# One-input POOL operations beside attention: normalising by a scalar, rounding for w3 and w_out, low parts on DVE

## The chip, the core and the metric

One core of a Trainium2 chip runs the whole kernel as one program. Five engines each work through their own list of instructions in order and wait for one another by semaphores: TensorE (PE, with weight loads listed as PEld), VectorE (DVE), ScalarE (ACT), GpSimd (POOL) and SyncE (SP), which here only starts DMAs. The metric is the device time of one execution in microseconds (us), smaller being better.

## The reference

Causal attention over 2 batches of 12 heads (448 positions, 64 wide), then two dense blocks on its 896 x 768 result:

```
scores = q @ k.T / 8, masked above the diagonal
x  = softmax(scores) @ v              # heads side by side: 896 x 768
h  = ((x @ w1) * (x @ w2)) @ w3 @ moe_w_out      # 768 -> 1024 -> 1024 -> 768
t  = h @ w_in                                    # 768 -> 2048
y  = (t * clip(t + 3, 0, 6) / 6) @ moe2_w_out    # 2048 -> 768
```

The weights arrive as 64-bit floating-point numbers and q, k, v are turned into 32-bit ones. The kernel has to return y in 32 bits.

## The kernel before, in words

**Weights.** A 64-bit weight is read as two 32-bit words, a high word (index 1) and a low word (index 0) side by side in a raw tile, `raw[:, :size, 0 or 1]`. `bits` (line 262) makes a 32-bit float of the pair in four steps: ACT scales the high words as floats (line 270); the top bits of the low words are brought down by 29 places, either on DVE by a shift (line 277) or, with `shifted`, on ACT by an activation with a scale and a bias (line 273); DVE merges the high words' mantissa bits (line 279) and then the sign bit (line 281). The 32-bit float stands in the low words' place, every other word of the tile. `split` (line 249) makes two parts of it: ACT rounds it to the format that TensorE multiplies fast (HI, line 252), and the difference from the unrounded value is the low part (LO, line 255). A product is then three multiplications, HI by HI, HI by LO and LO by HI.

**Units.** A unit is one 128-wide slice of a weight. For w3 (8 units of 1024 columns, tile `w3r`, parts `w`) and for moe_w_out, called wr (8 units of 768 columns, tile `wrr`, parts `wr`), the list `POOLED` puts the low part's subtraction on POOL; for the others it is on DVE. `convert` (line 284) does a unit, `fetch` (line 229) loads one. Three raw tiles and four tiles of parts go round; the wr parts have tiles of their own.

**Order of work.** The product w3 · moe_w_out ("pw", line 543, 16 half slices through `weights_product`) does not depend on attention and is run beside it. After it come eight steps "pa" that multiply x by w1 and w2 (line 686; `combine` forms sums of weight blocks for them, partly with two-input additions on POOL, line 320), then px (line 760), pg (line 625) and po (line 801).

**Attention** goes by 12 units of two heads, each in seven row tiles t = 6 … 0 of 64 · (t + 1) columns. For each tile PE forms scores (line 407), DVE masks them and takes the row bound (line 410), ACT takes the exponential and the row sum (line 414). `normalise` (line 419) is done in three groups (t = 6 and 5; 4 and 3; 2, 1 and 0): DVE adds a small constant to the sums and takes the reciprocal (lines 425, 426), and POOL multiplies each row tile by it (line 433). PE transposes the result in blocks (line 455), ACT and DVE copy it out (lines 463, 467), PE multiplies by v (line 480) and ACT and DVE write the parts of x (lines 497, 498).

**What sets the order.** A planner (`Plan.issue`) fixes each engine's order when the program is built: it plays the operations through with a price for each (`act`, `dve`, `pool`: a constant plus a price per column) and at each step gives an engine, among the operations that are ready, the one of lowest rank. Attention ranks by unit, conversion beside it by PACE · n, and pw at BESIDE + n, so that it fills in. The prices know nothing of one engine slowing another. What runs on the chip keeps the planned order even where the times turn out otherwise.

Of the kernel before, what the change touches and what calls it, by code (L numbers as in the profile page):

```python
# [14 lines left out]
ALU = mybir.AluOpType  # L15
# [18 lines left out]
POOLED = ("wr", "w3")  # L34
# [120 lines left out]
def attention_moe_moe2(ctx: ExitStack, tc, q, k, v, w1, w2, w3, w_out, v_in, v_out, out):  # L155
# [8 lines left out]
    nc = tc.nc  # L164
# [3 lines left out]
    P = 128  # L168
    T = 64
# [9 lines left out]
    HI, LO = 0, 1  # L179

    def f32(ap):
        return ap.bitcast(F32)
# [37 lines left out]
    def act(n, sb=False):  # L220
        return (0.29 if sb else 0.16) + n * 0.000833

    def dve(n):
        return 0.155 + n * 0.00104

    def pool(n):
        return 0.15 + n * 0.0023

    def fetch(plan, n, rank):
        if n >= len(units):  # L230
            return
        w, kt, m, name = units[n]
        size = kt * P
        if name == "w2":
            raw = plan.tile(lambda: later["t"].tile([P, KD * P, 2], U32, tag="raw2", name=f"{name}r{m}", bufs=2),
                            "raw2", 2, (done,))
            raw2s.append(raw)
        else:
            raw = plan.tile(lambda: ws.tile([P, KF * P, 2], U32, tag="raw", name=f"{name}r{m}", bufs=RAWS), "raw", RAWS)
        raws[n] = (raw, size)  # L240
        flat = lambda: raw[:, :size].rearrange("p f t -> p (f t)")
        if name == "wp":
            plan.op("sp", size * 0.0015, lambda: nc.sync.dma_start(flat()[:, :size], product_of[m].bitcast(U32)),
                    reads=[made], writes=[raw], rank=rank)
        else:
            plan.op("sp", size * 0.0029, lambda: nc.sync.dma_start(flat(), w[m].bitcast(U32)),
                    writes=[raw], rank=rank)

    def split(plan, hl, at_, size, x, reads, rank, eng="dve"):

        key = ("h", at_)
        plan.op("act", act(size, True), lambda: nc.scalar.copy(hl[:, HI, at_:at_ + size], x()),
                reads=reads, writes=[hl.at(("h", at_))], rank=rank)
        e = nc.gpsimd if eng == "pool" else nc.vector
        plan.op(eng, pool(size) if eng == "pool" else dve(size), lambda: e.tensor_tensor(  # L255
            hl[:, LO, at_:at_ + size], x(), f32(hl[:, HI, at_:at_ + size]), ALU.subtract),
            reads=[*reads, hl.at(("h", at_))], writes=[hl.at(("l", at_))], rank=rank)

    def parts(name, m):
        return plan.tile(lambda: ws.tile([P, 2, KF * P], F32R, tag="hl", name=f"{name}{m}", bufs=HLS), "hl", HLS)  # L260

    def bits(plan, raw, size, rank, shifted=False):

        hi = lambda: raw[:, :size, 1]
        lo = lambda: raw[:, :size, 0]
        hb, lb = raw.at("h"), raw.at("l")

        plan.op("act", act(size, True), lambda: nc.scalar.mul(hi().bitcast(F32), hi().bitcast(F32), 2.0 ** -112),  # L270
                writes=[hb], rank=rank)
        if shifted:
            plan.op("act", act(size, True), lambda: nc.scalar.activation(
                lo(), lo(), AF.Copy, bias=THIRD[1], scale=THIRD[0]), writes=[lb], rank=rank)
        else:
            plan.op("dve", 0.16 + size * 0.00052,
                    lambda: nc.vector.tensor_single_scalar(lo(), lo(), 29, ALU.logical_shift_right),
                    writes=[lb], rank=rank)
        plan.op("dve", dve(size), lambda: nc.vector.scalar_tensor_tensor(  # L279
            lo(), hi(), 3, lo(), ALU.logical_shift_left, ALU.bitwise_or), reads=[hb], writes=[lb], rank=rank)  # L280
        plan.op("dve", dve(size), lambda: nc.vector.scalar_tensor_tensor(  # L281
            lo(), hi(), 0x80000000, lo(), ALU.bitwise_and, ALU.bitwise_or), reads=[hb], writes=[lb], rank=rank)

    def convert(plan, n, rank):
        if n >= len(units):
            return
        w, kt, m, name = units[n]
        if name == "w1":
            return
        raw, size = raws.pop(n)  # L290
        if name == "w2":
            combine(plan, m, raws.pop(n - 1)[0], raw, rank)
            return
        if name == "wr":
            hl = plan.tile(lambda: wrp.tile([P, 2, KD * P], F32R, tag="wr", name=f"wr{m}", bufs=KF), "wr", KF)
        else:
            hl = parts(name, m)
        hls[n] = hl
        if name == "wp":
            x = lambda: f32(raw[:, :].rearrange("p f t -> p (f t)")[:, :size])  # L300
            split(plan, hl, 0, size, x, [raw], rank)
            return
        bits(plan, raw, size, rank)
        split(plan, hl, 0, size, lambda: f32(raw[:, :size, 0]), [raw.at("l")], rank,
              "pool" if name in POOLED else "dve")

    def combine(plan, f, r1, r2, rank):


        size, h = KD * P, KD * P // 2  # L310
        bits(plan, r1, size, rank, True)
        low = lambda r, i, k=1: f32(r[:, i * h:(i + k) * h, 0])
        high = lambda r, i, k=1: f32(r[:, i * h:(i + k) * h, 1])
        first, second, third, fourth = (parts(f"{c}", f) for c in ("wa", "wb", "wc", "wd"))
        split(plan, first, 0, size, lambda: low(r1, 0, 2), [r1.at("l")], rank)
        bits(plan, r2, size, rank, True)

        def add(eng, dst, reads, write, a, b, op):
            e = nc.gpsimd if eng == "pool" else nc.vector
            plan.op(eng, pool(h) if eng == "pool" else dve(h), lambda: e.tensor_tensor(dst(), a(), b(), op),  # L320
                    reads=reads, writes=[write], rank=rank)

        L1, L2, H1, H2 = r1.at("l"), r2.at("l"), r1.at("h"), r2.at("h")
        add(ADDS[0], lambda: high(r2, 0), [L2], H2, lambda: low(r2, 0), lambda: low(r2, 1), ALU.add)
        add(ADDS[1], lambda: high(r2, 1), [L1, L2], H2, lambda: low(r1, 0), lambda: low(r2, 0), ALU.subtract)
        add(ADDS[2], lambda: high(r1, 0), [L1, H2], H1, lambda: high(r2, 0), lambda: low(r1, 0), ALU.subtract)
        add(ADDS[3], lambda: high(r1, 1), [L1], H1, lambda: low(r1, 1), lambda: high(r1, 0), ALU.subtract)
        split(plan, third, 0, h, lambda: high(r1, 0), [H1], rank)
        split(plan, second, 0, size, lambda: high(r2, 0, 2), [H2], rank)
        split(plan, fourth, 0, h, lambda: low(r2, 1), [L2], rank)  # L330
        split(plan, fourth, h, h, lambda: high(r1, 1), [H1], rank)
        comb[f] = {"A11": (first, 0), "A12": (first, h), "S1": (second, 0), "S3": (second, h),
                   "S2": (third, 0), "A22": (fourth, 0), "S4": (fourth, h)}
# [8 lines left out]
    plan = Plan()  # L342
# [76 lines left out]
    def normalise(u, t0, t1):  # L419
        sm, pb = sums[u], pr[u]  # L420
        rank = u + (TQ - t0) * 0.05
        acc = [sm.at((1, t)) for t in range(t0, t1)]

        def go():
            nc.vector.tensor_tensor(sm[:, 2, t0:t1], sm[:, 1, t0:t1], small[:, :t1 - t0], ALU.add)
            nc.vector.reciprocal(sm[:, 1, t0:t1], sm[:, 2, t0:t1])  # L426

        plan.op("dve", 0.47, go, writes=acc, rank=rank)

        def scale(t):  # L430
            n = (t + 1) * T
            s = pb[:, OFF[t]:OFF[t] + n]
            nc.gpsimd.tensor_tensor(s, s, sm[:, 1, t:t + 1].to_broadcast([P, n]), ALU.mult)  # L433

        for t in reversed(range(t0, t1)):
            plan.op("pool", pool((t + 1) * T), lambda t=t: scale(t),
                    reads=[sm.at((1, t))], writes=[pb.at(t)], rank=rank)


# [86 lines left out]
    def ahead(n):  # L526
        beside = n + 2 <= last_beside
        fetch(plan, n + 3, PACE * (n + 3) if beside else DENSE + n)
        convert(plan, n + 2, PACE * (n + 2) + 1 if beside else DENSE + n + AHEAD)

    for n in range(KF + 2):
        fetch(plan, n, PACE * n)
        convert(plan, n, PACE * n + 1)
    fetch(plan, KF + 2, PACE * n)
    W = DM // 2
    def weights_product(i):
# [46 lines left out]
    for p in range(HK):  # L583
        x, b, b11, b21 = xt[p, 1], bf[p + HK], xt[p, 0], xt[p + HK, 0]
# [164 lines left out]
    n = after_jobs  # L749
# [3 lines left out]
    for m0 in range(0, KD, 2):  # L753
        group = [(m, b) for b in range(B) for m in (m0, m0 + 1)]
        ps = {g: bank("px%d_%d" % g) for g in group}
        for kk in range(KF):
            for m, b in group:
                def go(kk=kk, m=m, b=b, n=n + m - m0, ps=ps):
                    for a, c in ((HI, HI), (HI, LO), (LO, HI)):
# [5 lines left out]
                        writes=[ps[m, b]], rank=DENSE + n)  # L765
# [28 lines left out]
    for m in range(KD):  # L794
        po = [bank(f"po{m}_{b}") for b in range(B)]
        for half in range(2):
            for b in range(B):
                for kk in range(KF):
                    def go(ps=po[b], n=n, kk=kk, k=half * KF + kk, b=b):
                        for a, c in ((HI, HI), (HI, LO), (LO, HI)):  # L800
# [5 lines left out]
                            writes=[po[b]], rank=DENSE + n)  # L806
# [64 lines left out]
```

## Time and profile before

| | |
|---|---|
| median of 3 runs | 582.82 us (581.73 to 582.88) |
| profiled execution | 580.64 us, span from first to last instruction 578.9 us |
| PE, DVE, ACT, POOL busy in the span | 555.5, 401.4, 294.5, 150.2 us |
| chain that ended last | PE 72%, DVE 16%, POOL 4%, issue 4% |
| mean granted TensorE clock | 0.994 of full speed |

Busy time says how long an engine was in instructions, waiting inside an instruction included. The chain follows the last instruction back through whatever released each step. A row of grouped instructions gives count, busy time and mean duration, and then the idle time of the engine just before them with what ended it. A duration in the trace is that of one execution under the profiler.

### The profile page before, as it was taken

Reading aid. Unit: us, or ns where it says so; the run is one execution under the profiler, and the core shown is the slowest. Engines: PE = TensorE matmul, PEld = TensorE weight load, DVE = VectorE, ACT = ScalarE, POOL = GpSimd, SP = SyncE. Lnnn points to the kernel's source line nnn. Section 1 sums busy time; section 2 is a strip of 40 time slices with the busy share of each in tenths; the row PEclk is TensorE's granted clock in tenths of the full one; section 3 lists DMA queues with packets and bytes.
Section 4 is the critical chain, followed back from the end, with each engine's and each line's share of the span. In section 5 each row is a group of like instructions: output and inputs, shape, how many; then the busy total and the mean of one; then the engine's idle time right before and its main releaser. Section 6 shows DMA issues by size and latency. Waiting matters only on the chain.

```text
span 578.9 us, 7881 instructions
## 1 busy us (share of the span) xinstructions
PE 555.5 (96%) x2900; PEld 493.8 (85%) x2900; DVE 401.4 (69%) x675; ACT 294.5 (51%) x548; POOL 150.2 (26%) x143
## 2 busy tenths in 40 slices
PE   7697979899999999999999999999999999999997
PEld 5465656678899999889999999999999999999996
DVE  5979898897794799999736357877878855361000
ACT  5777778777673576665514335555555623130100
POOL 3968787697131243332100000000000000000000
PEclk9889999999999999999999999999999999999999
DMA  8655565543432233431413204333344442430000
GB/s 329 218 176 176 200 233 205 178 166 130 134 113 64 93 120 127 143 133 44 140 60 110 84 25 163 110 109 110 110 145 146 145 162 89 173 110 16 17 32 33
DMA packets 22855, 73.39 MB, mean 127 GB/s; under 512 B 2080, under 2 KB 11296, under 8 KB 20256
## 3 DMA queue, kind: packets, MB, share of 16 engines
q1 hardware_dynamic: 22816, 72.88, 36.6%
q8 instruction: 23, 0.38, 0.3%
q14 instruction: 16, 0.13, 0.1%
HBM read 66.98 MB, written 5.90 MB: 126 GB/s over the span
## 4 chain that ended last, share of the span: by engine, by line
PE 72%; DVE 16%; POOL 4%; issue 4%; DMA 2%; ACT 1%; SPq 0%; DVEq 0%; POOLq 0%; ACTq 0%
PE po L801 20%; PE pg L625 20%; PE px L760 10%; PE pw L543 9%; POOL prb L433 4%; PE s L407 3%; PE ptp L455 3%; PE paX L686 3%; DVE wd L255 2%; PE o L480 2%; DVE z L410 2%; DVE w1r L279 2%; PE paZ L686 1%; DMA ks<-in_k 1%; PE paY L686 1%
## 5 line engine op out<-in xcount | busy, mean ns | idle before, releaser
L801 PE MATMUL po<-g,vo 128*128 128x448 f32 x576 | 115.4, 362 | 0.0
L625 PE MATMUL pg<-x2t,vi 128*128 128x448 f32 x576 | 115.4, 362 | 0.0
L625 PEld LDWEIGHTS pg<-x2t,vi 128*128 128x128 f32 x576 | 108.0, 187 | 7.2
L801 PEld LDWEIGHTS po<-g,vo 128*128 128x128 f32 x576 | 108.0, 187 | 7.2
L433 POOL TENSOR_TENSOR prb<-prb,sums 128x448 f32<-128x448 f32 (+6 forms) x84 | 74.3, 911 | 27.5 <-DVE sums L426 25.3
L543 PE MATMUL pw<-wr,w 128*128 128x384 f32 x384 | 76.1, 347 | 0.5 <-POOL wr L255 0.5
L543 PEld LDWEIGHTS pw<-wr,w 128*128 128x128 f32 x384 | 65.9, 188 | 2.5 <-POOL wr L255 0.7
L407 PE MATMUL s<-ks,qs 128*128 128x448 f32 (+6 forms) x168 | 49.8, 405 | 10.5 <-DVE sums L410 9.8
L760 PE MATMUL px<-ab,wp 128*128 128x448 f32 x288 | 57.9, 362 | 0.0
L760 PEld LDWEIGHTS px<-ab,wp 128*128 128x128 f32 x288 | 54.0, 187 | 3.6
L414 ACT ACTIVATE prb<-z,sums 128x448 f32<-128x448 f32 (+6 forms) x84 | 42.3, 509 | 7.2 <-DVE sums L410 7.1
L407 PEld LDWEIGHTS s<-ks,qs 128*128 128x128 f32 x168 | 27.5, 192 | 19.3 <-DVE sums L410 14.2
L410 DVE CUSTOM_DVE_ANT_0 z<-s,maskb 128x448 f32<-128x448 f32 (+6 forms) x84 | 32.9, 418 | 11.5 <-PE s L407 7.3
L646 ACT ACTIVATE r<-pg,consts 128x448 f32<-128x448 f32 x32 | 20.3, 635 | 33.2 <-PE pg L625 33.2
L455 PEld LDWEIGHTS ptp<-ident,prb 128*128 128x128 f32 x192 | 23.0, 146 | 13.6 <-POOL prb L433 8.6
L455 PE MATMUL ptp<-ident,prb 128*128 128x128 f32 x192 | 27.8, 288 | 6.1 <-POOL prb L433 6.1
L270 ACT ACTIVATE vor<-vor 128x1024 f32<-128x1024 f32 x12 | 13.9, 1162 | 38.7 <-DMA vor<-in_moe_w_out 38.7
L463 ACT COPY pt<-ptp 128x512 f32<-128x512 f32 (+1 forms) x48 | 25.1, 563 | 16.0 <-PE ptp L455 15.8
L320 POOL TENSOR_TENSOR w2r<-w2r 128x384 f32<-128x384 f32 x8 | 11.4, 1431 | 77.7 <-DVE w2r L281 68.5
L648 DVE SCALAR_TENSOR_TENSOR g<-r,pg 128x448 f32<-128x448 f32 x32 | 19.8, 618 | 12.8 <-ACT r L646 12.6
L661 DVE COPY out<-po 128x448 f32<-128x448 f32 x6 | 3.8, 627 | 35.7 <-PE po L801 35.7
L659 ACT COPY out<-po 128x448 f32<-128x448 f32 x6 | 3.2, 536 | 46.1 <-PE po L801 28.3
(110 smaller groups left out, 922.6 us busy)
## 6 DMA issues: line engine op xcount, KB each, us to landing
vir<-in_moe_w_in SPq DMA_DIRECT2D x16, 768.0 KB, 4.2
vor<-in_moe_w_out SPq DMA_DIRECT2D x12, 1024.0 KB, 4.9
w3r<-in_moe_w SPq DMA_DIRECT2D x8, 1024.0 KB, 5.6
wrr<-in_moe_w_out SPq DMA_DIRECT2D x8, 768.0 KB, 4.9
w1r<-in_moe_w SPq DMA_DIRECT2D x8, 768.0 KB, 5.6
w2r<-in_moe_w SPq DMA_DIRECT2D x8, 768.0 KB, 4.3
qs<-in_q SPq DMA_DIRECT2D x12, 448.0 KB, 3.6
vr<-in_v SPq DMA_DIRECT2D x12, 256.0 KB, 2.7
```

Of the source, the lines that this page charges most:

```text
L407: plan.op("pe", pe4(n), lambda: nc.tensor.matmul(ps[:, :n], qs[u][:, t].rearrange("p h i -> p (h i)"), ks[u][:, :n], start=True, stop=True ...
L410: plan.op("dve", dve(n) + 0.09, lambda: nc.vector.tensor_tensor_reduce(out=z[:, :n], in0=ps[:, :n], in1=maskb[:, S - n:], scale=-SCALE, sc ...
L414: plan.op("act", act(n, True) + 0.2, lambda: nc.scalar.activation(pb[:, OFF[t]:OFF[t] + n], z[:, :n], AF.Exp, bias=sm[:, 0, t:t + 1], scal ...
L433: nc.gpsimd.tensor_tensor(s, s, sm[:, 1, t:t + 1].to_broadcast([P, n]), ALU.mult)
L455: nc.tensor.transpose(ps[:w, i * P:(i + 1) * P], pb[:, OFF[t] + kb * P:OFF[t] + kb * P + w], ident)
L463: plan.op("act", act(cut), lambda: nc.scalar.copy(dst()[:, :cut], ps[:, :cut]), reads=[ps], writes=[d.at((g, 0))], rank=rank)
L543: nc.tensor.matmul(ps[:, :W], weight(n, a, kk), hls[1 + kk][:, c, h * W:(h + 1) * W], start=kk == 0 and a == c, stop=kk == KF - 1 and a == LO)
L625: nc.tensor.matmul(ps[:, :S], weight(n, a, kk), x(kk, c), start=st, stop=sp)
L646: plan.op("act", act(S), lambda: nc.scalar.activation(r[:, :], ps[:, :S], AF.Relu, bias=three, scale=1.0), reads=[ps], writes=[r], rank=DE ...
L686: nc.tensor.matmul(ps[:, :S], hl[:, a, off + kk * P:off + (kk + 1) * P], t[:, c], start=first and kk == 0 and a == c, stop=kk == HK - 1 an ...
L760: nc.tensor.matmul(ps[m, b][:, :S], weight(n, a, kk), ab[kk][:, c, cols(b)], start=kk == 0 and a == c, stop=kk == KF - 1 and a == LO)
L801: nc.tensor.matmul(ps[:, :S], weight(n, a, kk), gt[k][:, c, cols(b)], start=k == 0 and a == c, stop=k == KF2 - 1 and a == LO)
```

## The change

Three things change, and the planner, which has a new price `single(n)`, orders all engines anew.

- `normalise` multiplies by a scalar per partition (`tensor_scalar`, with a second multiplication by 1.0) in place of a two-input multiplication with the reciprocal broadcast along the row.
- For w3 and wr, POOL forms HI, as a multiplication by 1.0 twice with the rounded format as output, where ACT made it. DVE forms LO, where POOL made it.
- For the same units the top bits of the low words come from ACT (line 273's form) where DVE shifted them, and the last bit operation on DVE writes its result densely to the front of the raw tile, over high and low words, where it wrote every other word.

```diff
+    def single(n):
+        return 0.27 + n * 0.00085
...
     def split(plan, hl, at_, size, x, reads, rank, eng="dve"):
-        key = ("h", at_)
-        plan.op("act", act(size, True), lambda: nc.scalar.copy(hl[:, HI, at_:at_ + size], x()),
+        if eng == "pool":
+            plan.op("pool", single(size), lambda: nc.gpsimd.tensor_scalar(
+                hl[:, HI, at_:at_ + size], x(), 1.0, 1.0, ALU.mult, ALU.mult),
                 reads=reads, writes=[hl.at(("h", at_))], rank=rank)
-        e = nc.gpsimd if eng == "pool" else nc.vector
-        plan.op(eng, pool(size) if eng == "pool" else dve(size), lambda: e.tensor_tensor(
+        else:
+            plan.op("act", act(size, True), lambda: nc.scalar.copy(hl[:, HI, at_:at_ + size], x()),
+                    reads=reads, writes=[hl.at(("h", at_))], rank=rank)
+        plan.op("dve", dve(size), lambda: nc.vector.tensor_tensor(
             hl[:, LO, at_:at_ + size], x(), f32(hl[:, HI, at_:at_ + size]), ALU.subtract),
...
+        to = (lambda: flat(raw)[:, :size]) if packed else lo
         plan.op("dve", dve(size), lambda: nc.vector.scalar_tensor_tensor(
-            lo(), hi(), 0x80000000, lo(), ALU.bitwise_and, ALU.bitwise_or), reads=[hb], writes=[lb], rank=rank)
+            to(), hi(), 0x80000000, lo(), ALU.bitwise_and, ALU.bitwise_or),
+            reads=[] if packed else [hb], writes=[lb, hb] if packed else [lb], rank=rank)
...
-        bits(plan, raw, size, rank)
-        split(plan, hl, 0, size, lambda: f32(raw[:, :size, 0]), [raw.at("l")], rank,
-              "pool" if name in POOLED else "dve")
+        pooled = name in POOLED
+        bits(plan, raw, size, rank, shifted=pooled, packed=pooled)
+        split(plan, hl, 0, size, lambda: f32(flat(raw)[:, :size] if pooled else raw[:, :size, 0]),
+              [raw.at("l")], rank, "pool" if pooled else "dve")
...
-            nc.gpsimd.tensor_tensor(s, s, sm[:, 1, t:t + 1].to_broadcast([P, n]), ALU.mult)
+            nc.gpsimd.tensor_scalar(s, s, sm[:, 1, t:t + 1], 1.0, ALU.mult, ALU.mult)
...
-            plan.op("pool", pool((t + 1) * T), lambda t=t: scale(t),
+            plan.op("pool", single((t + 1) * T), lambda t=t: scale(t),
```

## Rows read from the trace of the kernel before

**Rows 1.** Busy time by stretch: PE, PEld, DVE, ACT, POOL, PE clock, DMA share, GB/s
```profile
10.00:90.00 80.00, 66.08 (x374) 43.97 (x372) 70.65 (x187) 60.81 (x160) 63.05 (x61) 0.96 0.61 212
90.00:150.30 60.30, 57.51 (x358) 45.45 (x357) 51.67 (x121) 45.37 (x107) 44.91 (x39) 1.00 0.45 149
150.30:184.30 34.00, 34.00 (x196) 33.99 (x197) 27.74 (x35) 18.42 (x32) 9.38 (x5) 1.00 0.37 117
184.30:575.40 391.10, 389.88 (x1944) 363.74 (x1942) 248.02 (x319) 165.29 (x244) 29.81 (x20) 1.00 0.30 102
```
**Rows 2.** Waits: who waited for whom, us in total, times, longest
```profile
PE s L407 <- DVE sums L410: 9.8, 8, 2.2
PE ptp L455 <- POOL prb L433: 6.1, 7, 1.5
```
**Rows 3.** Chain of waits in order of time: start, us, what
```profile
17.88 2.70 POOL w L255
```
**Rows 4.** Costliest groups on the page: normalising on POOL, all 84
```profile
L433 POOL TENSOR_TENSOR prb<-prb,sums 128x448 f32<-128x448 f32 (+6 forms) x84 | 74.3, 911 | 27.5 <-DVE sums L426 25.3
```
**Rows 5.** Groups by shape on POOL, 93.7 to 96.0 us: normalising undisturbed
```profile
L433 POOL TENSOR_TENSOR prb<-prb,sums 128x448 f32<-128x448 f32 x1 | 0.9, 934 | 0.1
...
L433 POOL TENSOR_TENSOR prb<-prb,sums 128x64 f32<-128x64 f32 x1 | 0.3, 289 | 0.0
```
**Rows 6.** Line 255 on POOL: duration min/median/max in ns, first and last start
```profile
L255 POOL TENSOR_TENSOR w<-w3r,w x8: 2403/2486/3488, 17.8 to 152.6; 128x1024 fp32r<-128x1024 f32 x8
L255 POOL TENSOR_TENSOR wr<-wrr,wr x8: 1844/1857/2471, 27.0 to 80.0; 128x768 fp32r<-128x768 f32 x8
```
**Rows 7.** Groups by shape on POOL: operations with one input, in the setup
```profile
L388 POOL TENSOR_SCALAR_AFFINE_SELECT maskb<-maskb 64x448 f32<-64x448 f32 x2 | 1.1, 557 | 0.1
...
masks.py:199 POOL TENSOR_SCALAR_AFFINE_SELECT ident<-ident 128x128 f32<-128x128 f32 x1 | 0.3, 295 | 0.1
```
**Rows 8.** Timeline, 79.9 to 81.5 us: start, us, engine, line, operation
```profile
80.00 1.86 POOL L255 TENSOR_TENSOR wr<-wrr,wr 128x768 fp32r<-128x768 f32 x1
...
80.60 1.28 DVE L425 TENSOR_TENSOR sums<-sums,consts 128x3 f32<-128x3 f32 x1
```
**Rows 9.** Groups on DVE: busy us, mean ns of one, idle before
```profile
L279 DVE SCALAR_TENSOR_TENSOR w3r<-w3r 128x1024 uint32<-128x1024 uint32 x8 | 11.5, 1438 | 1.4 <-ACT w3r L270 1.4
L281 DVE SCALAR_TENSOR_TENSOR w3r<-w3r 128x1024 uint32<-128x1024 uint32 x8 | 10.8, 1356 | 0.0
L277 DVE TENSOR_SCALAR w3r<-w3r 128x1024 uint32<-128x1024 uint32 x8 | 9.2, 1150 | 0.0
L279 DVE SCALAR_TENSOR_TENSOR wrr<-wrr 128x768 uint32<-128x768 uint32 x8 | 10.0, 1245 | 1.3 <-ACT wrr L270 1.2
L281 DVE SCALAR_TENSOR_TENSOR wrr<-wrr 128x768 uint32<-128x768 uint32 x8 | 11.4, 1423 | 0.0
L277 DVE TENSOR_SCALAR wrr<-wrr 128x768 uint32<-128x768 uint32 x8 | 8.6, 1081 | 0.7 <-DMA wrr<-in_moe_w_out 0.7
L425 DVE TENSOR_TENSOR sums<-sums,consts 128x2 f32<-128x2 f32 (+1 forms) x36 | 13.8, 383 | 0.0
L277 DVE TENSOR_SCALAR vor<-vor 128x1024 uint32<-128x1024 uint32 x12 | 8.3, 694 | 20.6 <-DMA vor<-in_moe_w_out 20.6
L277 DVE TENSOR_SCALAR vir<-vir 128x768 uint32<-128x768 uint32 x16 | 9.0, 561 | 12.0 <-DMA vir<-in_moe_w_in 11.9
L255 DVE TENSOR_TENSOR vo<-vor,vo 128x1024 fp32r<-128x1024 f32 x12 | 14.7, 1223 | 14.4 <-ACT vo L252 14.4
L255 DVE TENSOR_TENSOR vi<-vir,vi 128x768 fp32r<-128x768 f32 x16 | 15.3, 954 | 1.1 <-ACT vi L252 1.1
```
**Rows 10.** Line 425 on DVE: duration min/median/max in ns, first and last start
```profile
L425 DVE TENSOR_TENSOR sums<-sums,consts x36: 144/201/1539, 9.6 to 140.6; 128x2 f32<-128x2 f32 x24, 128x3 f32<-128x3 f32 x12
```
**Rows 11.** Groups on ACT: the copy that leaves, the activation that comes
```profile
L273 ACT ACTIVATE w1r<-w1r 128x768 uint32<-128x768 uint32 x8 | 7.4, 930 | 0.0
...
L252 ACT CAST wr<-wrr 128x768 fp32r<-128x768 f32 x8 | 7.4, 921 | 2.7 <-DVE wrr L281 2.7
```

More of the change, by code (lines that the diff above doesn't have):

```diff
@@ L260, in parts, with flat, bits @@
         return plan.tile(lambda: ws.tile([P, 2, KF * P], F32R, tag="hl", name=f"{name}{m}", bufs=HLS), "hl", HLS)
-    def bits(plan, raw, size, rank, shifted=False):
+    def flat(raw):
+        return raw[:, :].rearrange("p f t -> p (f t)")
+    def bits(plan, raw, size, rank, shifted=False, packed=False):
         hi = lambda: raw[:, :size, 1]
@@ L299, in convert @@
         if name == "wp":
-            x = lambda: f32(raw[:, :].rearrange("p f t -> p (f t)")[:, :size])
+            x = lambda: f32(flat(raw)[:, :size])
             split(plan, hl, 0, size, x, [raw], rank)
             return
-        bits(plan, raw, size, rank)
-        split(plan, hl, 0, size, lambda: f32(raw[:, :size, 0]), [raw.at("l")], rank,
-              "pool" if name in POOLED else "dve")
+        pooled = name in POOLED
+        bits(plan, raw, size, rank, shifted=pooled, packed=pooled)
+        split(plan, hl, 0, size, lambda: f32(flat(raw)[:, :size] if pooled else raw[:, :size, 0]),
+              [raw.at("l")], rank, "pool" if pooled else "dve")
     def combine(plan, f, r1, r2, rank):
```

## The prediction

> **What bounds the kernel now.** I read the stage table first. From 150.3 us on TensorE is busy 423.9 of 425.1 us [rows 1]: behind attention nothing shortens the kernel but an earlier start of that part. Between 10 and 150.3 us, the attention with the product w3·w_out as filler, TensorE stands idle 80 − 66.08 + 60.3 − 57.51 = 16.7 us, and its mean granted clock of 0.96 from 10 to 90 us (some of it at the lower level) costs another 0.04 · 80 = 3.2 us [rows 1]. These 19.9 us are the ceiling of any gain here. Idle time before 10 us is the first loads and is not touched.
>
> Next, who ends TensorE's idle time: 9.8 us DVE (the score reduction has not yet emptied a score bank), 6.1 us POOL (rows not yet normalised) [rows 2]. DVE is the fullest engine up to 90 us, 70.65 of 80 us, and POOL is busy 63.05 [rows 1]; both work in order. The chain of waits tells the same early on: at 17.88 us it runs 2.70 us through the low part of the first w3 unit on POOL [rows 3], with the normalising that PE's transposes need queued behind it.
>
> Then why DVE is full. A three-element add on DVE takes 1.28 us, starting at 80.60 and ending at 81.88, while POOL runs a two-input subtraction from 80.00 to 81.86 [rows 8]. Its shortest record is 0.144 us, its longest 1.539 [rows 10]. So some DVE instructions stand still while POOL is in an instruction; this one reads SBUF on two streams. The same shows wherever an operation exists beside attention and after it: the shift of 1024 columns 1150 ns against 694, of 768 columns 1081 against 561, the two-input operations 1438 and 1356 against 1223, 1245 and 1423 against 954 (for the last three figures "after" is the low-part subtraction of the same size) [rows 9]. In sum DVE's waiting is 8·0.456 + 8·0.520 for the shifts, 8·(0.215 + 0.133) + 8·(0.291 + 0.469) for the two-input steps and 36·(0.383 − 0.144) for the small adds: 7.8 + 8.9 + 8.6 = 25.3 us.
>
> **The change part by part.**
> *Normalising* (84 instructions, 74.3 us with waits [rows 4]). Alone it takes 934 ns at 448 columns and 289 at 64 [rows 5], so 0.18 us + 1.68 ns a column, and 7·0.18 + 1792·1.68 ns = 4.27 us for the seven of a unit. The trace has no POOL operation with one tensor input and a scalar per partition. Its nearest one-input row is the affine select: 557 ns at 448, 295 at 128 [rows 7], 0.19 us + 0.82 ns a column, which gives 2.80 us a unit: the lower end. The upper end is today's 4.27, if the scalar pointer costs what the broadcast operand does. I take the planner's price in the diff, 7·0.27 + 1792·0.85 ns = 3.41, because its slope is that of the one-input row. An estimate.
>
> *High parts on POOL instead of low parts.* Removed: 8 subtractions of 1024 columns and 8 of 768, 2.40 and 1.84 us at the shortest [rows 6]. Added: 16 one-input multiplies. By the affine row 1.03 and 0.82 us; at worst as today. Taken as the planner has them: 1.14 and 0.92. POOL's work alone in this stage so goes from 12·4.27 + 8·2.40 + 8·1.84 = 85.1 us to 12·3.41 + 8·1.14 + 8·0.92 = 57.4 us (ends 48.4 and 85.1).
>
> *Low parts on DVE.* Added 8·1.223 + 8·0.954, removed shifts 8·0.694 + 8·0.561 (alone, [rows 9]): +7.4 us. Both kinds are of the sort that waits for POOL, so the number of such instructions stays at 84.
>
> *DVE's waiting.* An instruction that comes at a random moment waits (POOL's busy share) × (mean remainder of the POOL instruction, Σt²/2Σt). Before, over the 142 us from 10 us to the start of the last subtraction [rows 6]: 85.1/142 = 0.60, remainder 108.4/170.2 = 0.64, product 0.38 us; measured 25.3/84 = 0.30, so the estimate is to be scaled by 0.79. After: 57.4/142 = 0.40, remainder 38.1/114.8 = 0.33, scaled 0.106 us, times 84 = 8.9 us. Saved: 16.4. DVE nets −16.4 + 7.4 = −9.0 us of its 122.3 in the stage. With POOL's upper end the saving is nil and DVE has 7.4 us more work; with its lower end (0.34 · 0.29 · 0.79 · 84 = 6.5) it is 18.8.
>
> No row has a one-input POOL instruction beside such a DVE instruction. I take it that it holds DVE off as the two-input one does [rows 8], so that only its shorter length helps and the new subtractions stay among those that wait; if it holds nothing off, the waiting goes altogether (third rival).
> The Trainium skill, "SBUF — State Buffer", Who interferes with whom, has a rule that speaks against the change here: a DVE instruction with two SBUF inputs contends with any POOL instruction that reads SBUF, with one input as with two, and whichever starts first holds the shared ports for all its length. For two inputs the trace agrees (the add's 1.28 us); for one, nothing in it shows either. By the rule the sum is the 8.9 us of waiting above, without it none.
>
> *Shift on ACT instead of the rounding copy.* 16 copies leave (921 ns at 768 columns), 16 activations come (930 ns for the same [rows 11]): nothing in sum. They come right behind the scaling as a unit lands, so exps queue behind two passes rather than one. ACT is busy 60.81 of 80 us [rows 1] and three raw buffers give a unit time; I put it at nothing, and at 1 us if that cover is gone.
>
> *The packed output* of the last bit operation: same columns, same inputs, nothing. *DMAs*: same number and size; a raw buffer comes free after DVE's subtraction instead of POOL's, nothing.
>
> *The added wait.* DVE's subtraction now waits for POOL's high part, and behind it on DVE stand the score reductions (PE's banks) and the reciprocals, for which POOL's next normalising waits. The planner places the subtraction where its prices have POOL done, and these leave such waiting out. Mean excess: one POOL instruction's remainder at 40%, 0.13 us, up to a whole high part (about 1 us). I take 0.2 · 16 = 3.2 us of DVE time, half reaching PE.
>
> *The sum for TensorE.* Half of the idle time that DVE ends goes, since DVE's own slack up to 90 us (9.35 us) grows by more than half: 4.9. A third of POOL's, since a normalising group alone is 20% shorter and waits less often behind a long instruction: 2.0. Half of the clock's 3.2, on the view that fewer idle stretches leave TensorE less often at the lower level: 1.6. The new wait: −1.6. Together 6.9 us. That is 573.7 us by the profiled execution's 580.64 (span 578.9); the median of the runs shown lies 2.2 us above that execution, so 575.9 on it. The end of attention would come some 7 us earlier, with about as much of the product left. Between 150.3 and 184.3 DVE has 27.74 us of work (forming the next stage's operands) under 34.0 us of PE's leftover product [rows 1]; that covers it as long as the leftover shrinks by less than 6 us. Beyond, DVE would be late for the next stage, which is why I don't go higher.
>
> **Rivals.**
> *DVE in order behind POOL (slower).* If the 16 subtractions each stand 1.4 us (a high part and a neighbour's remainder), DVE loses 22.4 us against the 9.0 saved, 13.4 more than before; half of it on PE, 6.7, less the 2.0 from POOL: 587.5. It decides from 9.0/16 = 0.56 us a subtraction. For it: both queues are in order, the planner knows no such waiting, and each waits for the other in turn. Against: POOL has 28 us less work, and a unit's steps are interleaved with other units'. Chance 0.20.
> *PE takes nothing from it (same).* The order on PE is written by the planner; faster partners may only make idle time elsewhere, as filler runs out or the 27.74 us come due. 582.8. Chance 0.11.
> *One input does not exclude DVE (faster still).* All 25.3 us go and DVE nets −17.9, twice the forecast's; DVE's part of PE's idle time, 9.8, then goes whole, which adds 4.9: 571.0. For it: the instruction asks for one stream of reads where today's asks for two. Against: normalising takes 74.3 us where 12 · 4.27 = 51.2 alone would do [rows 4, 5], so POOL is held off by DVE as well, and an instruction of one input may be held off just so. Chance 0.12.
> *The one-input form costs what the broadcast does.* POOL falls only to 12·4.27 + 8·1.90 + 8·1.47 = 78.2 us; by the same product (0.55 · 0.52 · 0.79 · 84 = 19.0) DVE's waiting falls by 6.3 against 7.4 added. PE pays half of 1.1 and the new wait's 1.6: 585. Against: the affine row. Chance 0.07.
>
> **How the numbers follow.** Forecast 0.50 at 575.9, its own range 570 to 580.5. Faster is the forecast but for a little of its upper edge, and the third rival: 0.62. Same takes the second, that edge and part of the fourth: 0.14. Slower is the first and the rest: 0.24. About 0.2% (1.2 us) is what a measurement of this kernel can tell from no change. The range for 8 in 10 goes from 567, which takes in most of the third, to 585.5, which leaves out the worse half of the first.
>
> **What would show it.** Right: high parts on POOL at about 1.14 and 0.92 us alone; a normalising of 448 columns at 0.65; the small add near 0.2 us in the mean; DVE's two-input operations near their lengths alone; TensorE's idle time up to the end of attention near 10 us, the granted clock at 1 from 10 to 90. Wrong: DVE waiting for POOL's high part as a leading row in the waits; a POOL one-input operation above 1.5 us alone; or TensorE waiting for the next stage's operands after its leftover product.

## The result, and the profile after

The changed kernel takes 589.46 us in the median of 4 runs (588.85 to 591.99) against 582.66 for the kernel before in 4 runs; the ratio is 1.0141, 95% interval [1.0107, 1.0176]. It is slower by 6.8 us where 6.9 us of gain were forecast. The ratio on record is larger than the quotient of these two medians, 1.0117; by either the change is a loss. The profiled execution took 588.85 us, span 587.0 us, which is 8.2 us more than the profiled execution of the kernel before.

The stage table of the kernel after, beside [rows 1]; columns are PE, PEld, DVE, ACT and POOL busy, granted clock, DMA share, GB/s:

```profile
10.00:90.00 80.00, 67.67 (x375) 44.56 (x376) 60.00 (x195) 61.89 (x163) 47.38 (x64) 0.96 0.62 208
90.00:150.30 60.30, 54.05 (x314) 43.23 (x313) 42.10 (x108) 40.53 (x98) 35.85 (x36) 0.93 0.46 153
150.30:184.30 34.00, 34.00 (x194) 32.04 (x194) 28.61 (x39) 20.54 (x36) 8.94 (x5) 0.97 0.34 111
184.30:575.40 391.10, 389.83 (x1950) 364.27 (x1949) 248.82 (x320) 166.14 (x245) 29.75 (x20) 1.00 0.30 103
```

From 10 to 90 us DVE is busy 10.7 us less and POOL 15.7 us less, from 90 to 150.3 us 9.6 and 9.1 us less: the load fell as meant. TensorE still stands idle 12.3 + 6.3 = 18.6 us, 1.9 more than before, and loses more clock: 0.04·80 + 0.07·60.3 + 0.03·34 = 8.4 us against 3.2. Those two make 7.1 of the 8.2 us. What TensorE waits for has changed sides, beside [rows 2]:

```profile
PE ptp L468 <- POOL prb L446: 15.6, 9, 2.8
PE s L420 <- DVE sums L423: 2.0, 2, 1.5
```

DVE ends 2.0 us of it instead of 9.8, POOL 15.6 instead of 6.1. The groups that answer to [rows 4, 6, 5, 9] follow. Normalising, from the page of the kernel after:

```profile
L446 POOL TENSOR_SCALAR prb<-prb,sums 128x448 f32<-128x448 f32 (+6 forms) x84 | 70.0, 847 | 58.7 <-DVE sums L439 29.4
```
POOL's high parts in it (duration min/median/max in ns, first and last start):
```profile
L255 POOL TENSOR_SCALAR w<-w3r x8: 1038/1044/1522, 18.7 to 158.9; 128x1024 fp32r<-128x1024 f32 x8
L255 POOL TENSOR_SCALAR wr<-wrr x8: 825/826/829, 29.5 to 82.2; 128x768 fp32r<-128x768 f32 x8
```
Normalising undisturbed, a group by shape from 52.5 to 53.3 us:
```profile
L446 POOL TENSOR_SCALAR prb<-prb,sums 128x448 f32<-128x448 f32 x1 | 0.6, 632 | 0.0
```
And DVE's groups (busy us, mean ns, idle before):
```profile
L261 DVE TENSOR_TENSOR w<-w3r,w 128x1024 fp32r<-128x1024 f32 x8 | 10.1, 1266 | 3.9 <-POOL w L255 3.9
L288 DVE SCALAR_TENSOR_TENSOR w3r<-w3r 128x1024 uint32<-128x1024 uint32 x8 | 10.0, 1249 | 2.5 <-ACT w3r L282 1.7 <-DMA ks<-in_k 0.7
L292 DVE SCALAR_TENSOR_TENSOR w3r<-w3r 128x1024 uint32<-128x1024 uint32 x8 | 9.8, 1230 | 0.0
L438 DVE TENSOR_TENSOR sums<-sums,consts 128x2 f32<-128x2 f32 (+1 forms) x36 | 7.0, 194 | 0.9 <-ACT prb L427 0.9
```

DVE's two-input operations of 1024 columns now run nearly at their length alone (1230 to 1266 ns, alone 1223) and the small add at 194 ns instead of 383. Normalising alone fell from 934 to 632 ns at 448 columns; yet all 84 together fell only from 74.3 to 70.0 us. Alone they would take 12 · 3.31 = 39.7 us (the shortest record of each length, added up for a unit), so they wait 30 us on POOL, where before they waited 74.3 − 51.2 = 23.

Where that hurts is seen in the timeline of the kernel after (start, us, engine, line, operation, idle before):

```profile
141.56 1.20 DVE L261 TENSOR_TENSOR w<-w3r,w 128x1024 fp32r<-128x1024 f32 x1
141.82 4.74 POOL L446 TENSOR_SCALAR prb<-prb,sums 128x192 f32<-128x192 f32 x3 [0.39 <-DVE sums L439]
...
142.68 0.62 DVE L585 TENSOR_TENSOR xt<-bf,xt 128x448 f32<-128x448 f32 x1
...
143.33 0.65 DVE L585 TENSOR_TENSOR bf<-bf,xt 128x448 f32<-128x448 f32 x1
143.90 1.21 DVE L288 SCALAR_TENSOR_TENSOR w3r<-w3r 128x1024 uint32<-128x1024 uint32 x1
145.15 1.22 DVE L292 SCALAR_TENSOR_TENSOR w3r<-w3r 128x1024 uint32<-128x1024 uint32 x1
...
146.61 0.48 PE L468 MATMUL ptp<-ident,prb 128*128 128x128 f32 x1 [2.74 <-POOL prb L446]
```

("..." marks lines left out.) Five two-input operations follow one another on DVE, none more than 0.04 us over its shortest record. POOL's group of the three short row tiles (192, 128 and 64 columns, 1.10 us alone; from here on "the short group") lies beside them for 4.74 us; its three instructions end 0.21, 0.16 and 0.18 us after the second, fourth and fifth of DVE's. TensorE, whose next work in order is this unit's transposes, stands for 2.74 us. In the kernel before, the same group of the same unit, also beside two-input operations on DVE, was through in 3.08 us, and there DVE's were the lengthened ones:

```profile
141.19 3.08 POOL L433 TENSOR_TENSOR prb<-prb,sums 128x192 f32<-128x192 f32 x3 [0.38 <-DVE sums L426]
141.45 1.33 DVE L279 SCALAR_TENSOR_TENSOR w3r<-w3r 128x1024 uint32<-128x1024 uint32 x1 [0.41 <-ACT w3r L270]
...
142.81 1.31 DVE L281 SCALAR_TENSOR_TENSOR w3r<-w3r 128x1024 uint32<-128x1024 uint32 x1
...
144.04 0.71 DVE L572 TENSOR_TENSOR xt<-bf,xt 128x448 f32<-128x448 f32 x1
```

The granted clock falls at such gaps (same columns as the stage table):

```profile
90.00:100.00 10.00, 7.45 (x41) 6.77 (x39) 5.62 (x12) 5.45 (x14) 6.75 (x6) 0.83 0.56 177
140.00:150.00 10.00, 7.26 (x38) 6.84 (x37) 5.33 (x8) 4.86 (x9) 5.79 (x4) 0.79 0.30 100
150.00:160.00 10.00, 10.00 (x55) 8.04 (x54) 4.95 (x7) 6.58 (x12) 1.13 (x1) 0.87 0.29 98
```

TensorE stood 2.55 us up to 94.36 us and ran at the lower level (1.2 GHz) for 3.4 us from 94.65; it stood 2.74 us up to 146.61, and the lower level came within this gap, at 145.85, for 6.8 us. Up to 139 us attention is equally far in both kernels (unit 11 of 12 has its last attention multiplication done at 139.0 us after, 139.5 before), but the product that fills in is behind: 138 of its 384 multiplications have ended by then, 153 before. The last unit then is 5.6 us late, of which 1.7 is the longer group and about 3.4 the 6.8 us at the lower level, and the filling product ends at 192.0 us instead of 184.3.

### The profile page after: what moved, and what is told of

Its sections match the earlier page's. It is cut to its first block, busy times and chain, and to the rows that moved or that the text cites. A ratio compares the mean times of both kernels' runs of the same rounds, so it can differ in the third digit from the quotient of the medians.

```text
span 587.0 us, 7900 instructions
## 1 busy us (share of the span) xinstructions
PE 561.6 (96%) x2900; PEld 498.0 (85%) x2900; DVE 383.0 (65%) x675; ACT 293.4 (50%) x548; POOL 125.2 (21%) x143
## 4 chain that ended last, share of the span: by engine, by line
PE 79%; DVE 9%; POOL 3%; DMA 3%; issue 3%; ACT 2%; SPq 0%; DVEq 0%; POOLq 0%; ACTq 0%
PE po L814 20%; PE pg L638 20%; PE pw L556 10%; PE px L773 10%; PE s L420 5%; PE ptp L468 5%; PE paX L699 4%; PE o L493 4%; POOL prb L446 3%; DVE wd L261 2%; PE paZ L699 2%; DVE w1r L288 1%; DMA ks<-in_k 1%; PE paY L699 1%; DMA w1r<-in_moe_w 1%
## 5 line engine op out<-in xcount | busy, mean ns | idle before, releaser
L446 POOL TENSOR_SCALAR prb<-prb,sums 128x448 f32<-128x448 f32 (+6 forms) x84 | 70.0, 847 | 58.7 <-DVE sums L439 29.4
L556 PE MATMUL pw<-wr,w 128*128 128x384 f32 x384 | 78.1, 353 | 0.0
L556 PEld LDWEIGHTS pw<-wr,w 128*128 128x128 f32 x384 | 67.6, 194 | 1.5 <-issue 0.9
L468 PE MATMUL ptp<-ident,prb 128*128 128x128 f32 x192 | 30.3, 304 | 15.8 <-POOL prb L446 15.6
L468 PEld LDWEIGHTS ptp<-ident,prb 128*128 128x128 f32 x192 | 24.6, 154 | 22.7 <-POOL prb L446 18.2
L493 PEld LDWEIGHTS o<-pt,vr 128*64 128x64 f32 (+1 forms) x192 | 10.9, 134 | 19.1 <-issue 12.3
L493 PE MATMUL o<-pt,vr 128*64 128x448 f32 (+3 forms) x192 | 26.9, 396 | 0.0
```

What stands on the lines that cost most here:

```text
L446: nc.gpsimd.tensor_scalar(s, s, sm[:, 1, t:t + 1], 1.0, ALU.mult, ALU.mult)
L468: nc.tensor.transpose(ps[:w, i * P:(i + 1) * P], pb[:, OFF[t] + kb * P:OFF[t] + kb * P + w], ident)
L493: nc.tensor.matmul(ps[T * j:T * j + T, kb * P:S], vr[u][:w, kb, j, :], d[:w, base[kb]:base[kb] + TQ - 2 * kb, j, :], start=kb == 0, stop=k ...
L556: nc.tensor.matmul(ps[:, :W], weight(n, a, kk), hls[1 + kk][:, c, h * W:(h + 1) * W], start=kk == 0 and a == c, stop=kk == KF - 1 and a == LO)
```

## The experiments

Twelve kernels ran, in three sets of four beside the kernel before (581.33, 581.15 and 581.29 us; beside the changed kernel it was 582.66, so 1 or 2 us between kernels of different sets say nothing). Three parts of the change were switched apart: the weights' parts (high on POOL, low on DVE, shift on ACT), the form of normalising, and its price in the planner. The price changes no instruction, only the order. Where only the form differs between two kernels, their order is the same.

**First set.** Theories: A, the one-input form gives way to DVE and PE waits for the short group; B, the planner's new order is what costs, the form is harmless; C, the low parts moved to DVE are what costs.

e1, the form alone, in the order of before:
```diff
-            nc.gpsimd.tensor_tensor(s, s, sm[:, 1, t:t + 1].to_broadcast([P, n]), ALU.mult)
+            nc.gpsimd.tensor_scalar(s, s, sm[:, 1, t:t + 1], 1.0, ALU.mult, ALU.mult)
```


> Before with the one-input form of normalising alone, at the old price, so every engine keeps the order of before. Theory A (the one-input form gives way: DVE stops waiting for it, POOL waits instead, and PE waits for the last group of three short row tiles): DVE's small add in the mean near 0.2 us, that group over 2.08 us in the mean, time not better than before, 582 to 588. Theory B (the form is harmless, the order that the new prices make is what costs): shorter instructions in the old order, 575 to 580.

575.36 us, ratio 0.9897 [0.9871, 0.9923]: faster, as B said. PE's wait for POOL fell:
```profile
PE ptp L455 <- POOL prb L433: 4.7, 7, 1.5
```
The short group did not lengthen (2.10 us in the mean, before 2.08), and DVE's small add took 494 ns, not 0.2 us: low parts with two inputs were still on POOL, and some four fifths of DVE's waiting here is beside those. A fails as it was put: with the old weights and order the form does no harm.

e2, the form and its new price, weights as before:
```diff
+    def single(n):
+        return 0.27 + n * 0.00085
...
-            plan.op("pool", pool((t + 1) * T), lambda t=t: scale(t),
+            plan.op("pool", single((t + 1) * T), lambda t=t: scale(t),
```


> The one-input form of normalising with its new price, weights as before. Theory A: as e1 within 3 us, 582 to 589. Theory B: the new order shows already, 586 to 590, and at least 5 us over e1. Theory C (the low parts moved to DVE are what costs): no loss, 576 to 582.

578.48 us, ratio 0.9956 [0.9937, 0.9975]: 3.1 us over e1, by order alone. It lies in C's range; B wanted 586, A 582.

e3, the weights' parts alone (the changed kernel with the old form and price):
```diff
-            nc.gpsimd.tensor_scalar(s, s, sm[:, 1, t:t + 1], 1.0, ALU.mult, ALU.mult)
+            nc.gpsimd.tensor_tensor(s, s, sm[:, 1, t:t + 1].to_broadcast([P, n]), ALU.mult)
...
-            plan.op("pool", single((t + 1) * T), lambda t=t: scale(t),
+            plan.op("pool", pool((t + 1) * T), lambda t=t: scale(t),
```


> The change to the weights alone (high parts on POOL, low parts on DVE, shift on ACT), normalising by two inputs at the old price. Theory A: the short group stays near 2.1 us and POOL has 15 us less work, so 576 to 581. Theory C: 587 to 590, nearly all of the loss. Theory B: anything that is not near after, no figure.

578.78 us, ratio 0.9959 [0.9934, 0.9984]. C falls: the move by itself is a small gain. The time is in A's range, but the short group took 2.38 us, not the 2.1 that A said: the move lengthens it before the form does.

e4, the changed kernel with the old form only, in its own order:
```diff
-            nc.gpsimd.tensor_scalar(s, s, sm[:, 1, t:t + 1], 1.0, ALU.mult, ALU.mult)
+            nc.gpsimd.tensor_tensor(s, s, sm[:, 1, t:t + 1].to_broadcast([P, n]), ALU.mult)
```


> After with the two-input form of normalising at the new price, so every engine keeps the order of after. Theory A: the short group falls back from 2.62 to about 2.1 us, PE's gaps of 2.5 us before its transposes go, 580 to 585. Theory B: 588 to 592, the order has it all.

584.88 us, ratio 1.0041 [1.0015, 1.0067]: 6.1 us over e3 by the price alone, 4.6 under the changed kernel by the form alone. The time is in A's range but the gaps, which were to go, stayed:
```profile
PE ptp L468 <- POOL prb L446: 13.2, 10, 3.1
```
The profiled execution, 581.16 us, is the fastest of ten. From 10 to 150.3 us it idles 16.9 us on TensorE, only 1.7 less than the changed kernel, but up to 300 us it runs 3.4 us at the lower level where that runs 17.1; half of these 13.7 us is most of the 7.7 us between the two profiled executions. So the new price costs in both pairs, while the form gains 6 us with the old weights and loses 4.6 with the new ones. No single theory had that. The next set took the price as the theory, P.

**Second set.** e5, the changed kernel with the old price:
```diff
-            plan.op("pool", single((t + 1) * T), lambda t=t: scale(t),
+            plan.op("pool", pool((t + 1) * T), lambda t=t: scale(t),
```


> After with the planner's old price for normalising (0.15 + 2.3 ns a column) and nothing else changed; the engines' order is that of e3, the form that of after. Theory P (the new price, 0.49 us in the mean where one takes 0.85 on the chip, lets the planner place PE's transposes ahead of the filler too soon): PE's idle time before its transposes falls from 15.8 us to under 10, 572 to 580. Theory A (the one-input form gives way to DVE's added subtractions, whatever the order): 585 to 589, as after.

581.98 us, ratio 1.0007 [0.999, 1.0025]: 7.5 us under the changed kernel, but neither theory's range, and PE's wait stays high:
```profile
PE ptp L468 <- POOL prb L446: 12.1, 10, 3.1
```
Against e3, which has the same order, the one-input form makes the short group longer (2.38 to 2.61 us) and the kernel 3.2 us slower.

e6, the changed kernel with 0.85 us for each row tile, which is what one takes on the chip:
```diff
-            plan.op("pool", single((t + 1) * T), lambda t=t: scale(t),
+            plan.op("pool", 0.85, lambda t=t: scale(t),
```


> After with a price for normalising of 0.85 us for each row tile, whatever its length, which is what one takes in the mean in the trace of after. Theory P: as good as e5 or better, 570 to 579, and PE's idle time before its transposes lowest of all. Theory A: 584 to 589.

568.62 us, ratio 0.9782 [0.976, 0.9803]: the same instructions as the changed kernel, 21 us faster. Its stages (columns as above) and then PE's wait:
```profile
10.00:90.00 80.00, 73.06 (x421) 50.84 (x422) 69.17 (x212) 68.46 (x178) 54.73 (x69) 0.98 0.68 237
90.00:150.30 60.30, 60.30 (x377) 50.20 (x376) 50.16 (x113) 46.88 (x106) 30.14 (x32) 1.00 0.53 175
```
```profile
PE ptp L468 <- POOL prb L446: 1.4, 3, 0.8
```
The short group still takes 2.40 us and normalising as long on POOL (70.4 us for the 84, after 70.0); PE has its filler before the transposes instead of a gap, and idles 6.9 us from 10 to 150.3 us where the changed kernel idled 18.6.

e7, the short group on DVE:
```diff
-            nc.gpsimd.tensor_scalar(s, s, sm[:, 1, t:t + 1], 1.0, ALU.mult, ALU.mult)
+            e = nc.gpsimd if t1 > 3 else nc.vector
+            e.tensor_scalar(s, s, sm[:, 1, t:t + 1], 1.0, ALU.mult, ALU.mult)
...
-            plan.op("pool", single((t + 1) * T), lambda t=t: scale(t),
+            plan.op(*(("pool", single((t + 1) * T)) if t1 > 3 else ("dve", 0.16 + (t + 1) * T * 0.00052)), lambda t=t: scale(t),
```


> After with the three short row tiles of each unit multiplied on DVE, priced 0.16 us + 0.52 ns a column, the four long ones on POOL as in after. Theory A (the short group being held off on POOL is what costs): its 2.62 us go to under 1 us on DVE, PE's gaps of over 2.5 us go, 574 to 581. Theory P: the long groups are still priced too low, so at most half of the loss goes, 582 to 588.

568.4 us, ratio 0.9771 [0.9745, 0.9797], beyond what either theory gave. The long groups keep the low price, so this points to the short one as what cost, though POOL also has 36 instructions less here. On DVE its tiles take 344 ns in the mean:
```profile
L447 DVE TENSOR_SCALAR prb<-prb,sums 128x192 f32<-128x192 f32 (+2 forms) x36 | 10.7, 344 | 0.4
```

e8, the kernel before with the new price only:
```diff
+    def single(n):
+        return 0.27 + n * 0.00085
...
-            plan.op("pool", pool((t + 1) * T), lambda t=t: scale(t),
+            plan.op("pool", single((t + 1) * T), lambda t=t: scale(t),
```


> Before with the new price for normalising and nothing else: its form, the weights and all instructions as before, only the order of the engines new. Theory P: PE's idle time before its transposes rises by some 4 us, as from e1 to e2 and from e3 to e4, 584 to 588. Theory A: no loss, 580 to 583.

583.12 us, ratio 1.002 [0.9996, 1.0043]: the interval does not exclude no change, and the time lies between the two ranges. PE's wait for POOL rose by the 4 us that P said (from 6.1, [rows 2]); DVE's part fell from 9.8 to 5.1:
```profile
PE ptp L458 <- POOL prb L436: 9.9, 8, 2.2
```

**Third set.** Is it the price alone, without the change?

e9, the kernel before, priced at the mean of its own trace:
```diff
-            plan.op("pool", pool((t + 1) * T), lambda t=t: scale(t),
+            plan.op("pool", 0.91, lambda t=t: scale(t),
```


> Before with the planner's price for normalising set to 0.91 us for each row tile, which is the mean in its own trace (the old price has a mean of 0.74); every instruction as before. Theory P1 (the gain of e6 is the price's alone): 570 to 575. Theory P2 (a right price helps, but the gain needs the change's lighter load on POOL and its shorter waits on DVE): 576 to 582.

582.69 us, ratio 1.0024 [1.0004, 1.0043]. No gain: P1 falls, and the time lies above P2's range too. PE's wait for POOL before its transposes is gone and its wait for DVE, still held off by POOL's two-input instructions, is larger than before:
```profile
PE s L407 <- DVE sums L410: 14.9, 14, 2.8
```

e10, e1 with the price 0.85:
```diff
-            plan.op("pool", pool((t + 1) * T), lambda t=t: scale(t),
+            plan.op("pool", 0.85, lambda t=t: scale(t),
```


> Before with the one-input form of normalising, priced 0.85 us for each row tile; the weights as before. Theory P1: 569 to 573. Theory P2: between e1 (575.4) and e6 (568.6); if it reaches 570 the move of the weights' parts is worth under 2 us with a right price.

574.54 us, ratio 0.9878 [0.9847, 0.991], where P2 had it. With a fitting price the form is worth 8.2 us (against e9) and the move of the weights' parts another 5.9 (e6).

e11, the changed kernel's price raised by a constant:
```diff
-            plan.op("pool", single((t + 1) * T), lambda t=t: scale(t),
+            plan.op("pool", 0.36 + single((t + 1) * T), lambda t=t: scale(t),
```


> After with normalising priced at 0.63 us + 0.85 ns a column: the slope of the change's price, the mean (0.85 us) of e6. If the level of the price is what counts: 568 to 573. If e6's gain lies in the short tiles' price being raised most, which are the ones held off: 575 to 582.

571.44 us, ratio 0.9829 [0.9808, 0.9851]. The level brings 18 of the 21 us, and PE's wait is as short as in e6:
```profile
PE ptp L468 <- POOL prb L446: 1.0, 2, 0.5
```

e12, e7 with 0.85 for the long tiles:
```diff
-            plan.op(*(("pool", single((t + 1) * T)) if t1 > 3 else ("dve", 0.16 + (t + 1) * T * 0.00052)), lambda t=t: scale(t),
+            plan.op(*(("pool", 0.85) if t1 > 3 else ("dve", 0.16 + (t + 1) * T * 0.00052)), lambda t=t: scale(t),
```


> e7 (short row tiles multiplied on DVE) with the long ones, still on POOL, priced 0.85 us each. If the two repairs remove different waits: 564 to 567. If both remove the same wait, PE's before its transposes, which e6 and e7 have brought to about 2 us: 567 to 570.

570.09 us, ratio 0.9812 [0.9791, 0.9834], at the upper end of the second range: together the two repairs bring nothing over either, so they remove the same wait.

**All together.** The short group's length on the chip (first start to last end, mean of 12 units), its price (the planner's for its three tiles, 384 columns in all), the first less the second as the excess, and PE's wait for POOL before transposes (e9 has no such wait). In the three sets the kernel before had 581.2 to 581.3 us; its 582.7 stands beside the changed kernel's 589.5:

| kernel | weights | form | on chip, us | price, us | excess | PE waits, us | median, us |
|---|---|---|---|---|---|---|---|
| e9 | old | two | 2.09 | 2.73 | −0.64 | none | 582.7 |
| e10 | old | one | 2.26 | 2.55 | −0.29 | 1.3 | 574.5 |
| e6 | new | one | 2.40 | 2.55 | −0.15 | 1.4 | 568.6 |
| e11 | new | one | 2.16 | 2.22 | −0.06 | 1.0 | 571.4 |
| before | old | two | 2.08 | 1.33 | 0.75 | 6.1 | 582.7 |
| e1 | old | one | 2.10 | 1.33 | 0.77 | 4.7 | 575.4 |
| e8 | old | two | 2.17 | 1.14 | 1.03 | 9.9 | 583.1 |
| e3 | new | two | 2.38 | 1.33 | 1.05 | 9.2 | 578.8 |
| e2 | old | one | 2.19 | 1.14 | 1.05 | 8.2 | 578.5 |
| e4 | new | two | 2.33 | 1.14 | 1.19 | 13.2 | 584.9 |
| e5 | new | one | 2.61 | 1.33 | 1.28 | 12.1 | 582.0 |
| after | new | one | 2.62 | 1.14 | 1.48 | 15.6 | 589.5 |

Up to small inversions PE's wait rises with this excess, whatever the weights and the form. The excess of the two long groups does not order the waits: in e5 these are under their price by 0.60 and 0.36 us and PE waits 12.1 us, in e7 they are over it by 0.78 and 0.13 and no wait of PE is put down to POOL. And in the changed kernel all nine waits end within 0.06 us of the end of the short group's last tile. The time has two more parts: TensorE's idle time that DVE ends, and the clock.

## Why the prediction was wrong

**Bound and ceiling: right.** From 184.3 to 575.4 us TensorE is busy 389.9 us before and 389.8 after; what was won or lost lies in front of that. e6 gained 12.5 us of the 19.9.

**DVE's load: right, and more than forecast.** 8.9 us of waiting were forecast; measured are 36 · (0.194 − 0.143, its shortest record) for the small adds and about 1 us for the others, so some 3 us. The high parts' lengths alone were mis-sized by a tenth (1.04 and 0.826 us for 1.14 and 0.92), normalising at 448 columns by 3% (0.632 for 0.651). DVE's share of PE's idle time fell by 7.8 us where 4.9 were forecast.

**The step that failed: "A third of POOL's, since a normalising group alone is 20% shorter and waits less often behind a long instruction: 2.0."** It rose by 9.5 us. Two things are missing from the step. First, the working counted only DVE's waiting for POOL. POOL's for DVE, 23 us in the trace of before, is named in the third rival and is no term of the sum. Three short instructions in a row can meet DVE's operations three times; the short group got longer (2.08 to 2.62 us, with the weights' part of the change alone 2.38) although its instructions alone got shorter, and it stands directly before PE's transposes. Second, the price was read only as the length of an instruction. It is also what places PE's filler: at 1.14 us for a group that takes 2.62 the transposes came too early in PE's list, and PE, in order, stood before them with filler behind them. e6 and e11 show this: from the changed kernel they differ by the price only, and PE's wait goes from 15.6 us to 1.4 and 1.0.

**Half of the clock's 3.2: wrong in sign.** It became 8.4. In the changed kernel's trace TensorE ran 17.1 us at the lower level before 300 us, in four stretches, in e6 3.4. In or just before each of the four stands a wait of PE for POOL of 1.6 to 2.7 us, but two more such waits, of 2.8 and 2.5 us, have no such stretch behind them.

**The added wait: larger than taken, and not the cause.** DVE waited for POOL's high parts 3.9 + 1.6 = 5.5 us; 3.2 were taken. No wait of PE in the changed kernel is put down to these low parts on DVE.

**The rivals.** "DVE in order behind POOL" had the nearest time (587.5) by a mechanism that did not occur: at 5.5/16 = 0.34 us a subtraction it stays under its own point of decision. "PE takes nothing" named the planner's order, but as a gain that is not taken; it was a loss. "One input does not exclude DVE" was nearly true of normalising and brought no gain: DVE waited some 22 us less, as this rival had it, while POOL's own waiting rose from 23 to 30 us, in front of PE's transposes. "The one-input form costs what the broadcast does" is out: 0.632 us alone at 448 columns against 0.934. (The working has two upper ends for POOL's work, 85.1 us and this rival's 78.2; the forecast uses neither.)

**What is shown, and what is argued.** Shown: the price's effect (e6, e11 against the changed kernel; e3 to e4, e5 to after, e1 to e2), that PE's waits end with the short group and go when it leaves POOL (e7), and that a price at the mean of the trace brings nothing without the change (e9). Argued from the overlaps and not tried by itself: that the form lengthens the short group only with the new weights (e3 to e5, e4 to after; not before to e1, e8 to e2) because DVE then has 16 more two-input operations and POOL nothing left that holds DVE off for long. No run changes the price of the short group alone, and none takes the three parts of the move of the weights (high parts on POOL, shift on ACT, packed output) one by one. How far the clock would fall with the gaps made otherwise was not tried.

## What to carry to other kernels

A price in a written-out or planned order is a forecast of when the result is there, waiting included, not the length of the instruction alone. When an operation is made cheaper, read from the new trace what it takes in place, above all for groups of short instructions directly in front of the engine that bounds the kernel, and set the price by that: here the same instructions took 589.5 us or 568.6. It is no gain by itself: the kernel before, priced at its own trace's mean, gained nothing (e9). And count a contention from both sides before booking a saving on one.

## What the runs showed of the hardware that was not expected

A short one-input POOL instruction hardly holds off DVE, but DVE holds it off. In the changed kernel 51 two-input DVE instructions met a normalising one; they took 0.04 us longer than alone in the mean, 0.43 at most. In the kernel before, 55 that met the two-input normalising took 0.26 us longer. Beside POOL's high parts (768 or 1024 columns, also one input) ten in e6 took 0.43 us longer, beside its two-input subtractions 19 in e1 took 0.75 us longer, up to 1.99. An instance with POOL first:

```profile
62.49 1.90 POOL L446 TENSOR_SCALAR prb<-prb,sums 128x448 f32<-128x448 f32 x2 [1.46 <-PE ptp L468]
62.91 1.03 DVE L292 SCALAR_TENSOR_TENSOR wrr<-wrr 128x768 uint32<-128x768 uint32 x1
```

DVE starts while the first of the two (0.64 us) runs and takes 1.03 us, against 0.93 to 0.95 mostly; POOL's second, 0.58 us alone, ends only after DVE's, 1.29 us long. The rule of the Trainium skill ("SBUF — State Buffer", Who interferes with whom) that whoever starts first has the shared ports for all its length fits the two-input instructions and POOL's waiting; for short one-input POOL instructions the measurement decides against it on DVE's side. Whether length or the scalar pointer makes the difference between normalising and the high parts, which both have one input, was not separated.
